# Copying transposed q and k out of PSUM in the order of the destination

## The chip, the cores and the metric

The kernel runs on one core of a Trainium2 chip. The metric is the device time of one execution in microseconds (us); several executions are timed and their median is compared.

## The reference

Two attentions over the same q, k and v (8 batches, 8 heads, 576 tokens, head size 64) are added, and the sum goes through a small network with a gated activation. One attention works on means of four neighbouring tokens (144 of them), the other only looks at keys fewer than 4 positions away.

```python
q_d = q.reshape(B, H, Sd, 4, D).mean(axis=3)          # k_d, v_d alike
out_d = sm_attn(q_d, k_d, v_d)
out_up = np.repeat(out_d, 4, axis=2)
mask = np.abs(pos[:, None] - pos[None, :]) < 4
scores = np.where(mask, scale * np.matmul(q, k.transpose(0, 1, 3, 2)), -1e9)
...
attn_out = out_up + out_local
x = attn_out.transpose(0, 2, 1, 3).reshape(B * S, H * D)   # 4608 x 512
h = x @ w_in                                               # 512 x 2048
return (h * (1 / (1 + np.exp(-h)))) @ w_out                # 2048 x 512
```

## The kernel before

**Work items.** The 64 heads are handled as 32 pairs (the two heads of a pair lie on partitions 0 to 63 and 64 to 127). For each pair p these tasks run:

- loads of q, k and v by SP's DMA queue; the tile `qs` holds six consecutive tokens per partition on 96 partitions;
- `cast`, to bf16 (`qb`, `kb`), on GpSimd (POOL), for the first four pairs on VectorE (DVE) and ScalarE (ACT);
- T (`ph_T`): TensorE (PE) transposes q in six pieces of 96 tokens into one PSUM bank and k into the neighbouring bank of a `duo` tile. Piece c holds the tokens 6g + c for g from 0 to 95, so the columns in PSUM stand in another order than the tokens. One VectorE instruction (L353) copies q to `qT`, one ScalarE instruction (L354) copies k to `kT`, both bf16 in SBUF, and both put the tokens in order on the way;
- `do_mean` (L362, L364), on VectorE: sums of two and then of four tokens of `qT` and `kT`, for the small attention;
- S1 and S2: scores by TensorE, and exponentials by ScalarE (L376, L391, L393);
- `do_mask` (L399), on VectorE;
- Z, once for two pairs: the sums of the exponentials on TensorE, copied to `zc` (ACT L423), sent by DMA into another shape (`zr`), inverted (`rr`, DVE L433), sent by DMA to DRAM (`scr`) and read back, broadcast over the partitions, as `Rb`. Pairs 2 and 3 take a direct way instead (L471);
- PV: the weighted values on TensorE, multiplied by `Rb` on VectorE (L488, L490) and added into `xT` (L507).

The network runs in 9 blocks of 512 tokens: g1 (TensorE into `hps`, then tanh on ScalarE at L530, then L532 on VectorE, which writes `gT`) and g2 (TensorE into `ops`, copied by ScalarE at L551, stored by SP). The two `duo` tiles are taken in turn by T, S1, S2, Z and PV; `hps` and `ops` have two buffers each.

**Order.** A planner in Python writes the order of each engine's instructions before the launch. It gives every operation a cost in nanoseconds, and always takes the next task that is ready by those costs; L353 and L354 are planned with 800 and 700. On the chip each engine then runs its list in that order, and waits on semaphores where an operand comes from another engine or a DMA.

Of the kernel before, what the change touches and what calls it, by code (L numbers as in the profile page):

```python
# [8 lines left out]
BF16 = mybir.dt.bfloat16  # L9
# [168 lines left out]
def bass_hourglass_attn__then__act_silu_kernel(  # L178
# [9 lines left out]
    with kctx:  # L188
# [4 lines left out]
        def R(name, psum=False):  # L193
            if name not in res:
                res[name] = Res(name, psum)
            return res[name]

        def sb(name, shape, dt, n=1):
            ts = [E(nc.sbuf_tensor(f"{name}{i}", shape, dt)) for i in range(n)]
            return ts if n > 1 else ts[0]  # L200
# [19 lines left out]
        qT = sb("qT", [128, S_], BF16, 2)  # L220
        kT = sb("kT", [128, S_], BF16, 2)
# [105 lines left out]
        def next_duo():  # L327
            d = nph[0] % 2
            nph[0] += 1
            return duo[d], [R(f"duo{d}a", True), R(f"duo{d}b", True)]  # L330
# [10 lines left out]
        def ph_T(p):  # L341
            D, bk = next_duo()
            j = p % 2
            for x, (nm, st) in enumerate((("q", qb), ("k", kb))):
                tps = D[:, x, 0:288].bitcast(BF16)
                for c in range(6):
                    w = st[j][:, c, :, :].rearrange("p h d -> p (h d)")
                    P.op("PE", lambda t, c=c, w=w, tps=tps: t.transpose(  # L348
                        tps[:, 96 * c:96 * c + 96], w, id_bf[:, :]),
                        r=[R("id"), R(f"{nm}b{j}")], w=[bk[x]], cost=42)  # L350
            src = [D[:, x, 0:288].bitcast(BF16).rearrange("p (r g) -> p r g", r=6) for x in range(2)]
            dst = [t[j][:, :].rearrange("p (g r) -> p r g", r=6) for t in (qT, kT)]
            P.op("DVE", lambda e: e.tensor_copy(dst[0], src[0]), r=[bk[0]], w=[R(f"qT{j}")], cost=800)  # L353
            P.op("ACT", lambda e: e.activation(dst[1], src[1], AF.Copy), r=[bk[1]], w=[R(f"kT{j}")], cost=700)  # L354

# [236 lines left out]
        for p in range(NPAIR):  # L592
            i, j, m, n, u = p % NST, p % 2, p % NP_, p % NVB, p % NR
# [22 lines left out]
            elif p % 2 == 1:  # L616
                task(side, f"r{z}", "DVE", [f"Z{z}"], [R(f"zr{z % 2}")], [], lambda z=z: do_recip(z))
                task(side, f"b{z}", chain(z), [f"r{z}", nm("PV", p - 1 - NR), nm("PV", p - NR)],
                     [R(f"scr{z % 2}")], [R(f"Rb{(p - 1) % NR}"), R(f"Rb{u}")], lambda z=z: do_bcast(z))
            task(attn, f"T{p}", "PE", [f"c{p}", nm("S2", p - 2)], [R(f"qb{j}"), R(f"kb{j}")], duo_w,  # L620
                 lambda p=p: ph_T(p))
            task(attn, f"S1{p}", "PE", [f"T{p}", nm("PV", p - NP_)], [R(f"qT{j}"), R(f"kT{j}")], duo_w,
                 lambda p=p: ph_S1(p), "row")
# [80 lines left out]
        while attn or side or g2n[0] < 16 * NSUP:  # L704
# [10 lines left out]
            if ready:  # L715
                ready.sort(key=lambda c: (c[2][6] != mode[0], c[1]))
                t = ready[0][2]
# [56 lines left out]
```

## Time and profile before

| | us |
|---|---|
| median of 3 runs (lowest to highest) | 443.34 (441.7 to 447.06) |
| the profiled execution | 443.05 |
| its span, first to last instruction | 441.0 |
| busy in the span: PE, DVE, ACT, POOL | 357.3, 329.6, 236.9, 157.7 |
| mean clock granted to TensorE, as a share of full speed | 0.965 |

Busy shares over the whole span mix three parts: a start of about 60 us without the network, a middle in which both attentions and the network run side by side, and an end from about 320 us on which holds little but the network. They are read apart, by windows.

### The profile page before, as it was taken

The page shows a single profiled execution, that of the slowest core. Times are in us where ns is not written, and L with a number is a line of the kernel's source. Part 1 is how long each engine was busy: PE and PEld are TensorE (multiplying, and loading weights), DVE is VectorE, ACT ScalarE, POOL GpSimd, SP SyncE. Part 2 cuts the span into 40 slices and gives each one's busy share as a digit, 9 for nine tenths or more (in the row PEclk, how much of TensorE's full clock was granted, in tenths as well). Part 3 has the DMA queues.
Part 4 walks back from the last instruction along what each step waited for, and adds up shares of the span by engine and source line. Part 5 has one row for each costly group of instructions (what it writes and reads, how often), then busy time and mean ns, then how long its engine had stood idle before and what let it go on. Part 6 is the DMA issues. An engine that isn't in the chain of part 4 may idle for free.

```text
span 441.0 us, 6955 instructions
## 1 busy us (share of the span) xinstructions
PE 357.3 (81%) x2688; PEld 211.4 (48%) x2688; DVE 329.6 (75%) x469; ACT 236.9 (54%) x328; POOL 157.7 (36%) x181
## 2 busy tenths in 40 slices
PE   3332278686859868889789989999999999999997
PEld 2211154352446544455445555555556555555553
DVE  5998399659789998999999999999966634333330
ACT  5830246623748638747468686767654243434331
POOL 4591637406354543262762746445110000000000
PEclk9999998978958999989999999999999999999999
DMA  6999999946756796484879887653205110010111
GB/s 182 229 304 298 205 210 230 220 120 167 197 133 149 210 216 161 143 210 124 205 164 230 207 209 175 194 175 87 92 27 159 51 48 25 24 49 24 48 49 71
DMA packets 81086, 66.38 MB, mean 151 GB/s; under 512 B 47006, under 2 KB 70558, under 8 KB 81054
## 3 DMA queue, kind: packets, MB, share of 16 engines
q1 hardware_dynamic: 75480, 57.38, 52.2%
q0 software_dynamic: 4224, 6.29, 5.9%
q10 hardware_dynamic: 1350, 2.28, 2.1%
q8 instruction: 21, 0.34, 0.4%
q14 instruction: 11, 0.09, 0.1%
HBM read 58.25 MB, written 9.61 MB: 154 GB/s over the span
## 4 chain that ended last, share of the span: by engine, by line
PE 46%; DVE 34%; ACT 10%; DMA 5%; issue 3%; ACTq 1%; POOL 1%; POOLq 0%
PE hps L338 21%; PE ops L338 19%; DVE qT L353 8%; DVE gT L532 6%; DVE hs L362 5%; ACT kT L354 5%; PE duo L338 4%; DVE Pt L399 3%; ACT th L530 3%; DVE xT L507 3%; DVE xo L488 3%; DVE qd L364 2%; DMA Rb<-scr 2%; PE duo L348 2%; DVE kd L364 1%
## 5 line engine op out<-in xcount | busy, mean ns | idle before, releaser
L338 PE MATMUL hps<-xT,w_in_sb 128*128 128x512 f32 x576 | 180.7, 441 | 10.9 <-DVE gT L532 10.5
L532 DVE SCALAR_TENSOR_TENSOR gT<-th,hps 128x512 bf16<-128x512 f32 x144 | 97.6, 687 | 73.1 <-ACT th L530 73.0
L338 PE MATMUL ops<-w_out_bf,gT 128*128 128x512 bf16 x576 | 149.3, 389 | 0.0
L530 ACT ACTIVATE th<-hps 128x512 f32<-128x512 f32 x144 | 88.9, 623 | 103.2 <-PE hps L338 96.8
L338 PEld LDWEIGHTS hps<-xT,w_in_sb 128*128 128x128 f32 x576 | 109.0, 196 | 46.2 <-DVE gT L532 12.2
L354 ACT ACTIVATE kT<-duo 128x576 bf16<-128x576 bf16 x32 | 67.8, 2120 | 23.8 <-DVE qT L353 12.4
L338 PEld LDWEIGHTS ops<-w_out_bf,gT 128*128 128x128 bf16 x576 | 47.3, 99 | 68.2 <-issue 26.3
L353 DVE COPY qT<-duo 128x576 bf16<-128x576 bf16 x32 | 66.6, 2082 | 2.9 <-PE duo L348 2.9
L317 POOL CAST vb<-vs 128x640 bf16<-128x640 f32 x32 | 27.0, 845 | 70.7 <-PE duo L338 46.5
L312 POOL CAST qb<-qs 96x768 bf16<-96x768 f32 x28 | 25.3, 903 | 74.7 <-PE duo L348 69.7
L319 POOL TENSOR_TENSOR vt<-vq 72x512 f32<-72x512 f32 x32 | 43.1, 1348 | 11.2 <-DMA vq<-in_v_dram 11.2
L338 PE MATMUL duo<-qT,kT 64*128 64x112 bf16 (+1 forms) x320 | 22.1, 233 | 21.9 <-ACT kT L354 9.5
L376 ACT ACTIVATE Pt<-duo 128x912 bf16<-128x912 f32 x32 | 30.9, 965 | 8.3 <-PE duo L338 7.6
L551 ACT ACTIVATE osb<-ops 128x512 f32<-128x512 f32 x36 | 21.7, 604 | 23.2 <-PE ops L338 19.6
L507 DVE TENSOR_TENSOR xT<-xo 128x576 fp32r<-128x576 f32 (+2 forms) x40 | 31.7, 808 | 1.1
L321 POOL TENSOR_TENSOR vd<-vt 72x256 bf16<-72x256 f32 x32 | 29.4, 918 | 4.1
L338 PEld LDWEIGHTS duo<-qT,kT 64*128 64x128 bf16 x320 | 11.7, 101 | 39.0 <-issue 13.2
L399 DVE TENSOR_TENSOR Pt<-Pt,mask_bf 128x1152 bf16<-128x1152 bf16 x32 | 28.9, 904 | 1.5 <-ACT Pt L391 1.5
L391 ACT ACTIVATE Pt<-duo 128x240 bf16<-128x240 f32 x32 | 12.4, 388 | 29.5 <-PE duo L338 23.8
L348 PE MATMUL duo<-id_bf,qb 96*128 96x96 bf16 x192 | 15.6, 225 | 14.4 <-POOL xo L273 4.8
L488 DVE TENSOR_TENSOR xo<-duo,Rb 128x456 f32<-128x456 f32 x32 | 19.9, 623 | 8.6 <-DMA Rb<-scr 7.6
L312 POOL CAST kb<-ks 96x768 bf16<-96x768 f32 x28 | 24.5, 877 | 1.7 <-DMA ks<-in_k_dram 1.7
(49 smaller groups left out, 273.5 us busy)
## 6 DMA issues: line engine op xcount, KB each, us to landing
vs<-in_v_dram SPq DMA_DIRECT2D x64, 160.0 KB, 4.2
qs<-in_q_dram SPq DMA_DIRECT2D x32, 288.0 KB, 4.9
ks<-in_k_dram SPq DMA_DIRECT2D x32, 288.0 KB, 5.6
vq<-in_v_dram SPq DMA_DIRECT2D x32, 288.0 KB
out_dram<-osb SPq DMA_DIRECT2D x36, 256.0 KB, 2.2
Rb<-scr SPq DMA_DIRECT2D x48, 180.0 KB, 3.6
w_in_sb<-in_moe_w_in_dram POOLq DMA_DIRECT2D x4, 1024.0 KB, 12.2
Rb<-scr ACTq DMA_DIRECT2D x12, 180.0 KB, 3.7
```

Of the source, the lines that this page charges most:

```text
L312: pool(lambda g, d=dst, s=src: g.tensor_copy(d, s), r=[R(f"{nm}s{i}")], w=[R(f"{nm}b{j}")], cost=830)
L319: pool(lambda g: g.tensor_tensor(vt[:, :, :], vq[i][:, :, 0:128], vq[i][:, :, 128:256], ALU.add), r=[R(f"vq{i}")], w=[R("vt")], cost=1290)
L321: pool(lambda g: g.tensor_tensor(vd[m][:, :, :], vt[:, :, 0:64], vt[:, :, 64:128], ALU.add), r=[R("vt")], w=[R(f"vd{m}")], cost=750)
L338: return P.op("PE", lambda t: t.matmul(out_, lhsT, rhs, start=start, stop=stop, skip_group_check=True), r, w, cost=cost)
L353: P.op("DVE", lambda e: e.tensor_copy(dst[0], src[0]), r=[bk[0]], w=[R(f"qT{j}")], cost=800)
L354: P.op("ACT", lambda e: e.activation(dst[1], src[1], AF.Copy), r=[bk[1]], w=[R(f"kT{j}")], cost=700)
L376: P.op("ACT", lambda e: e.activation(Pt[m][:, :, 0:456], D[:, :, 0:456], AF.Exp, scale=0.125), r=bk, w=[R(f"P{m}")], cost=930)
L399: P.op("DVE", lambda e: e.tensor_tensor(Pt[m][:, :, :], Pt[m][:, :, :], mask_bf[:, :].unsqueeze(1).to_broadcast([128, 2, S_]), ALU.mult), ...
L488: P.op("DVE", lambda e: e.tensor_tensor(xo[x][:, 0:456], D[:, 0, 0:456], Rb[u][:, 0:456], ALU.mult), r=[bk[0], R(f"Rb{u}")], w=[R(f"xo{x}" ...
L507: P.op("DVE", lambda e, dst=dst, in0=in0, in1=in1: e.tensor_tensor(dst, in0, in1, ALU.add), r=[R(f"xo{x}")], w=xblk(kc, t, e_), cost=180 + n)
L530: P.op("ACT", lambda e: e.activation(th[tb][:, :], hps[hb][:, :], AF.Tanh, scale=0.5), r=[R(f"h{hb}", True)], w=[R(f"th{tb}")], cost=600)
L532: P.op("DVE", lambda e: e.scalar_tensor_tensor(gT[j % 2][:, f, :], th[tb][:, :], 1.0, hps[hb][:, :], ALU.add, ALU.mult), r=[R(f"h{hb}", Tr ...
```

## The change

The two copies take the same elements to the same places; only the order in which an instruction walks through them differs. Before, the loop ran over the six pieces outside and the 96 tokens of a piece inside: consecutive elements are neighbours in PSUM (2 bytes apart), and land six elements (12 bytes) apart in SBUF. After, it runs over the 96 groups outside and the six pieces inside: consecutive elements are 96 elements (192 bytes) apart in PSUM and neighbours in SBUF. The planned costs are the same, and so each engine's list is the same, instruction for instruction; only the shapes of these two operands differ.

```diff
-            src = [D[:, x, 0:288].bitcast(BF16).rearrange("p (r g) -> p r g", r=6) for x in range(2)]
-            dst = [t[j][:, :].rearrange("p (g r) -> p r g", r=6) for t in (qT, kT)]
+            src = [D[:, x, 0:288].bitcast(BF16).rearrange("p (r g) -> p g r", r=6) for x in range(2)]
+            dst = [t[j][:, :].rearrange("p (g r) -> p g r", r=6) for t in (qT, kT)]
             P.op("DVE", lambda e: e.tensor_copy(dst[0], src[0]), r=[bk[0]], w=[R(f"qT{j}")], cost=800)
             P.op("ACT", lambda e: e.activation(dst[1], src[1], AF.Copy), r=[bk[1]], w=[R(f"kT{j}")], cost=700)
```

## Rows read from the trace of the kernel before

**Rows 1.** The page: busy times, then busy tenths in 40 slices of 11 us.

```profile
PE 357.3 (81%) x2688; PEld 211.4 (48%) x2688; DVE 329.6 (75%) x469; ACT 236.9 (54%) x328; POOL 157.7 (36%) x181
...
PE   3332278686859868889789989999999999999997
...
DVE  5998399659789998999999999999966634333330
...
DMA  6999999946756796484879887653205110010111
```

**Rows 2.** Windows of the span: busy us by engine, granted clock, DMA share, GB/s.

```profile
core 0: us, PE busy (x) PEld busy (x) DVE busy (x) ACT busy (x) POOL busy (x), PEclk, DMA share, GB/s
0.00:60.00 60.00, 17.81 (x219) 11.94 (x219) 44.00 (x55) 23.59 (x26) 32.40 (x51) 1.00 1.06 242
60.00:100.00 40.00, 32.61 (x209) 20.59 (x210) 30.43 (x41) 23.74 (x33) 18.00 (x21) 0.87 0.91 192
100.00:140.00 40.00, 28.91 (x273) 16.55 (x271) 34.62 (x44) 22.68 (x28) 20.30 (x21) 0.79 0.70 174
140.00:200.00 60.00, 49.79 (x425) 30.24 (x424) 55.73 (x82) 37.46 (x52) 26.84 (x30) 0.97 0.69 174
...
60.00:260.00 200.00, 164.26 (x1373) 98.46 (x1374) 178.06 (x247) 124.58 (x167) 96.14 (x102) 0.92 0.76 183
260.00:320.00 60.00, 57.92 (x503) 33.52 (x503) 56.91 (x91) 41.62 (x57) 27.44 (x28) 1.00 0.54 149
```

**Rows 3.** The page: the chain that ended last, shares of the span by line.

```profile
PE hps L338 21%; PE ops L338 19%; DVE qT L353 8%; DVE gT L532 6%; DVE hs L362 5%; ACT kT L354 5%; PE duo L338 4%; DVE Pt L399 3%; ACT th L530 3%; DVE xT L507 3%; DVE xo L488 3%; DVE qd L364 2%; DMA Rb<-scr 2%; PE duo L348 2%; DVE kd L364 1%
```

**Rows 4.** The two copies: durations in ns, min/median/max, first and last start.

```profile
L353 DVE COPY qT<-duo x32: 2016/2089/2122, 5.5 to 313.8; 128x576 bf16<-128x576 bf16 x32
...
L354 ACT ACTIVATE kT<-duo x32: 2082/2125/2154, 6.8 to 313.3; 128x576 bf16<-128x576 bf16 x32
```

**Rows 5.** Groups by shape: contiguous reads of PSUM on ACT and DVE (busy us, mean ns).

```profile
L376 ACT ACTIVATE Pt<-duo 128x912 bf16<-128x912 f32 x32 | 30.9, 965 | 8.3 <-PE duo L338 7.6 <-issue 0.3
...
L393 ACT ACTIVATE Pd<-duo 72x576 bf16<-72x576 f32 x32 | 20.5, 642 | 0.0
L488 DVE TENSOR_TENSOR xo<-duo,Rb 128x456 f32<-128x456 f32 x32 | 19.9, 623 | 8.6 <-DMA Rb<-scr 7.6 <-PE duo L338 1.0
...
L490 DVE TENSOR_TENSOR xo<-duo,Rb 128x264 f32<-128x264 f32 x32 | 13.4, 420 | 0.0
L391 ACT ACTIVATE Pt<-duo 128x240 bf16<-128x240 f32 x32 | 12.4, 388 | 29.5 <-PE duo L338 23.8 <-PE ops L338 3.7 <-PE duo L348 1.9
```

**Rows 6.** PE's waits from 60 to 260 us: total us, times, longest us.

```profile
PE hps L338 <- DVE gT L532: 9.7, 9, 3.3
PE duo L338 <- DVE xo L488: 7.5, 3, 3.1
PE duo L338 <- DVE qT L353: 6.5, 7, 3.1
PE duo L348 <- DVE qT L353: 3.9, 3, 1.7
...
PE duo L338 <- ACT kT L354: 1.5, 2, 0.9
```

**Rows 7.** Groups by shape on DVE from 60 to 260 us.

```profile
L353 DVE COPY qT<-duo 128x576 bf16<-128x576 bf16 x21 | 43.9, 2088 | 1.6 <-PE duo L348 1.6
```

**Rows 8.** Timeline of DVE in the start: start us, duration us, instruction, idle before.

```profile
5.51 2.08 DVE L353 COPY qT<-duo 128x576 bf16<-128x576 bf16 x1 [0.82 <-PE duo L348]
...
23.06 2.07 DVE L353 COPY qT<-duo 128x576 bf16<-128x576 bf16 x1
...
52.23 0.63 DVE L488 TENSOR_TENSOR xo<-duo,Rb 128x456 f32<-128x456 f32 x1 [7.59 <-DMA Rb<-scr]
```

**Rows 9.** Timeline of ACT and DVE: one round of denominators, from its copy to its use.

```profile
138.30 0.77 ACT L423 ACTIVATE zc<-duo 128x720 f32<-128x720 f32 x1
...
155.21 0.62 DVE L488 TENSOR_TENSOR xo<-duo,Rb 128x456 f32<-128x456 f32 x1
```

## Prediction

> **What bounds the kernel now.** I read the busy shares first, then windows, then the chain of waits, then PE's own waits. The slices [rows 1] show three parts. In the first five slices PE is busy a third of the time or less, DVE often 9 tenths, and the DMA engines 9 tenths nearly all the time. From there to about slice 28 DVE stands at 9 with few exceptions, and PE at 6 to 9. In the last eleven slices PE is at 9 and DVE at 3: that end is pure matrix work, holds no copy of q or k (the last starts at 313.8 us, [rows 4]), and the change can't touch it.
>
> The windows put numbers to this [rows 2]. From 60 to 260 us PE is busy 164.3 of 200 us (82%) and DVE 178.1 (89%); from 260 to 320 us PE is busy 57.9 of 60 (96.5%), so that this piece is already bound by TensorE although DVE has 56.9. What can be won lies mainly between 60 and 260 us, where PE idles 35.7 us. PE's waits there [rows 6] nearly all end on DVE: on `gT` 9.7 us, on the first product of PV 7.5, on the copy of q itself 6.5 + 3.9, and on ScalarE's copy of k only 1.5. DVE is in order and late, so whichever of its instructions PE needs is late; it is the bound of this stretch. The chain that ended last agrees [rows 3]: 8% of the span on L353 and 5% on L354, together 57 of 441 us.
>
> **The copies, one by one.** A copy of 576 elements takes 2089 ns on DVE and 2125 ns on ACT [rows 4]. What would it take at the full rate? From the contiguous reads of PSUM [rows 5]: on DVE 456 elements take 623 ns and 264 take 420, so (623 - 420) / 192 = 1.057 ns an element and 141 ns fixed, and 576 would take 750 ns. On ACT (965 - 388) / 672 = 0.859 ns an element and 182 ns fixed, so 677 ns. Turned round, the present copies cost (2089 - 141) / 576 = 3.38 ns an element on DVE and (2125 - 182) / 576 = 3.37 on ACT. Two engines with different rates of their own meet the same figure: the limit lies in how a memory is walked, not in the engine. The one odd thing about these instructions is the write of 2 bytes in every 12. That it is the write is my reading; no row shows a contiguous bf16 read of PSUM, so the read isn't cleared by itself.
>
> After the change the write is contiguous. The row for such a write is ACT's exponential into `Pd`: 576 bf16 elements a partition in 642 ns [rows 5], full rate. The read then steps 192 bytes, and no row shows a stepped read of PSUM. Its bounds: 750 and 677 ns if the step is free; as much as now, or more, if it costs what the stepped write costs. I take the lower end, since contiguous PSUM reads of several lengths all run at the engine's own rate, and both engines reach it. The saving is then 1.34 us of DVE and 1.45 us of ACT for each pair.
>
> [...]
>
> **The sum.** The profiled execution took 443.05 us, 2.05 outside its span, and the median of the runs is 443.34; I count from 443.05.
>
> *60 to 260 us.* 21 copies of q start here [rows 7], and as many of k. DVE's busy time falls by 21 x 1.339 = 28.1 to 149.9 us. If DVE kept its share of 89%, the stretch would last 168.4 us. But PE would then be busy 164.3 / 168.4 = 97.5%, more than the 96.5% of the densest stretch; at 96.5% it lasts 170.2 us. PE becomes the bound. I take 95.5%, 172 us, since the waits on `gT`, which come through ScalarE's tanh, won't all go. That is a gain of 28 us. ACT gives back 21 x 1.45 = 30 us of 124.6, but PE hardly waits on it, so I add nothing. The bounds of this term: at the least the waits that end on the copies themselves, 6.5 + 3.9 + 1.5 = 11.9 us; at the most all idle time and some clock. The granted clock was 0.87, 0.79 and 0.97 from 60 to 100, 100 to 140 and 140 to 200 us [rows 2]. [...]
>
> *260 to 320 us.* PE idles 2.1 us; I take nothing.
>
> *0 to 60 us.* Four copies of q, from 5.51 to 23.06 us, lie on DVE ahead of the first denominators [rows 8], 4 x 1.34 = 5.4 us. Behind them stand three transfers one after another, and the first product starts only at 52.23 us, after DVE idled 7.6 us for one of them, while the DMA engines are busy 9 tenths [rows 1]. An earlier start of a transfer into full engines comes back in part; between 0 and 5.4 I take 3.
>
> Sum: 28 + 3 = 31, so **412 us**. The chain gives a check from above: 35.3 us of L353 shrinks by 64%, 22.1 us of L354 by 68%, together 37.6 if nothing else came last; 31 is some four fifths of it. With the ends of each term (17 from 60 to 260 us if PE only gets to 90%, and 43 there) this case alone spans 396 to 425.
>
> **The rivals.** *A stepped read that costs part of it.* For it: consecutive elements are never neighbours in PSUM after the change. Against: nothing in the rows, they hold no such read. Halfway between the ends a copy takes 1420 ns and saves 0.67: DVE falls by 14.1 to 164.0 us, 184.3 us at its 89%, a gain of 15.7, and 1.5 in the start: 426 us, with 420 to 432 around it.
>
> *The denominators' round takes over.* From `zc` to the product that uses it 16.9 us go by in one round [rows 9], mostly transfers that a faster copy doesn't shorten. Some ten rounds lie between 60 and 260 us; 172 us give each 17.2. For it: that is close. Against: in 60 to 260 us PE's listed waits are on DVE's products late in DVE's list, and `Rb` held DVE back only in the start. If rounds come to 18 us, the stretch lasts 180: with 2 in the start, 421 us. It decides from rounds over 17.2 us on.
>
> *Nothing happens.* The 3.4 ns belong to 2-byte elements out of PSUM and not to the order of the write. For it: no row shows bf16 read out of PSUM in another way. 443 us.
>
> *Slower: the stepped read costs more than the stepped write.* A hop of 192 bytes at each element instead of 12. At 5 ns an element a copy takes 3.02 us, 0.93 more; 21 of them are 19.6 us on the engine that bounds the stretch, 22 us at its 89%, and 4 x 0.93 in the start: 469 us. It decides at 2.4 us a copy (0.32 more, some 9 us in all), 3.9 ns an element. Against: a walk through one bank of PSUM would have to be worse than one through SBUF.
>
> **How the numbers follow.** A measurement of this kernel tells about 2% from no change, so faster means below 434.5 us and slower above 452.2. Chances: forecast 0.60, partial price 0.17, denominators 0.07, nothing 0.09, slower 0.07. Faster is the first three but for a tail of 0.01: 0.83; the same 0.10; slower 0.07. The range takes the first three cases but for the thin end below 399 (much of the lower clock recovered) and leaves out the last two: 399 to 431.
>
> **What would show it.** L353 and L354 near 750 and 680 ns (right), near 1.4 us (the second case), unchanged or above 2.4 us (the last two). PE from 60 us to the last copy at 93% or more, with its waits on L353 gone and the rest short; a last copy of q near 283 us instead of 314; the pure end as long as before. If DVE idles on `Rb` or `zr` in many rounds, the third case holds. The forecast is wrong at its root if the copies fall to 750 ns and PE's share stays near 82%: then DVE was not the bound that I take it for.

## Result, and the profile after

The change makes the kernel faster: 421.82 us (421.47 to 422.9, 4 runs) against 443.94 us (441.7 to 447.06, 4 runs), a ratio of 0.950 with a 95% interval of 0.944 to 0.956. The forecast was 412 us, with 399 to 431 around it. The sign and the mechanism were right, the size was not: 21.2 us between the two profiled executions (443.05 and 421.84 us) where 31 were worked out.

The two copies first, in the kernel after (durations in ns, min/median/max, first and last start):

```profile
L353 DVE COPY qT<-duo x32: 683/750/758, 5.5 to 293.3; 128x576 bf16<-128x576 bf16 x32
...
L354 ACT ACTIVATE kT<-duo x32: 642/650/656, 6.7 to 292.8; 128x576 bf16<-128x576 bf16 x32
```

They answer to [rows 4]. The medians are 750 ns on DVE and 650 on ACT, where 750 and 677 were worked out from contiguous reads of f32: with a step of 192 bytes in PSUM the copies run at that rate.

The page of the kernel after, busy times, slices and chain:

```profile
PE 351.5 (84%) x2650; PEld 214.0 (51%) x2688; DVE 295.3 (70%) x469; ACT 195.6 (47%) x328; POOL 158.9 (38%) x181
...
PE   3503286868859969999799999999999999999996
...
DVE  5955799559788888998987989979948334333320
...
DMA  7999999967667795596979896733323100101011
...
PE 61%; DVE 15%; DMA 12%; ACT 4%; issue 3%; SPq 2%; ACTq 2%; POOL 1%; POOLq 0%
PE hps L338 27%; PE ops L338 25%; PE duo L338 6%; DMA Rb<-scr 5%; PE duo L348 4%; DMA scr<-rr 4%; DMA zr<-zc 3%; DVE hs L362 3%; DVE xT L507 2%; DVE xo L488 2%; DVE gT L532 2%; DVE qd L364 1%; ACT th L530 1%; ACTq L427 1%; DVE kd L364 1%
```

Against [rows 1] PE gets up to 9 from about slice 13 on, but the first twelve slices look much as before. L353 and L354 have gone from the chain of [rows 3]; in their place stand PE's own work and the three transfers of the denominators, 12% together.

To compare equal work, the span is cut where the network begins (60.92 us before, 54.53 after) and where the last copy of q begins (313.79 and 293.26). Windows before, then after; columns as in [rows 2]:

```profile
0.00:61.00 61.00, 18.81 (x231) 12.94 (x231) 44.97 (x57) 23.71 (x26) 32.40 (x51) 1.00 1.06 241
61.00:314.00 253.00, 215.78 (x1806) 128.27 (x1805) 228.07 (x328) 161.71 (x218) 122.14 (x127) 0.94 0.72 176
314.00:441.00 127.00, 122.72 (x655) 70.24 (x654) 56.52 (x87) 51.47 (x85) 3.19 (x3) 1.00 0.16 56
```

```profile
0.00:54.50 54.50, 18.56 (x230) 12.83 (x231) 37.87 (x56) 16.88 (x26) 31.72 (x49) 1.00 1.07 249
54.50:293.40 238.90, 211.03 (x1782) 130.91 (x1806) 201.69 (x328) 128.49 (x218) 124.08 (x130) 0.94 0.79 191
293.40:419.80 126.40, 121.89 (x644) 70.30 (x654) 55.75 (x87) 50.23 (x85) 3.10 (x3) 1.00 0.16 57
```

The start gave 6.5 us, the middle 14.1 and the end 0.6. In the middle PE idles 27.9 us of 238.9 where it idled 37.2 of 253; DVE is busy 84% of it, so it isn't the bound all along any more. The starts of the copies of q (numbered from 0) show where the middle's gain came. From copy 5 to copy 9 the stretch went from 39.2 us (61.65 to 100.89) to 40.2 (57.41 to 97.59): nothing gained. From copy 9 to copy 31 it went from 213.0 to 195.8 us: 17.2 gained over 22 copies, where 22 x 1.34 = 29.5 us were taken off DVE.

What DVE does in the stretch that gained nothing, on its timeline in the kernel after, with GpSimd's behind it (start us, duration us, instruction, idle before):

```profile
66.25 1.95 DVE L364 TENSOR_TENSOR qd<-hs 128x144 bf16<-128x144 f32 x1
68.12 2.21 DVE L362 TENSOR_TENSOR hs<-kT 128x288 f32<-128x288 bf16 x1
70.37 2.92 DVE L364 TENSOR_TENSOR kd<-hs 128x144 bf16<-128x144 f32 x1
...
90.18 0.59 DVE L433 RECIPROCAL rr<-zr 40x72 f32<-40x72 f32 x1 [1.62 <-DMA zr<-zc]
...
93.46 0.31 DVE L364 TENSOR_TENSOR qd<-hs 128x144 bf16<-128x144 f32 x1
```

```profile
68.75 1.27 POOL L319 TENSOR_TENSOR vt<-vq 72x512 f32<-72x512 f32 x1
70.10 0.83 POOL L321 TENSOR_TENSOR vd<-vt 72x256 bf16<-72x256 f32 x1
70.88 0.81 POOL L312 CAST qb<-qs 96x768 bf16<-96x768 f32 x1
71.64 0.82 POOL L312 CAST kb<-ks 96x768 bf16<-96x768 f32 x1
72.41 0.71 POOL L317 CAST vb<-vs 128x640 bf16<-128x640 f32 x1
```

An addition of 144 elements takes 0.31 us at 93 us, with GpSimd idle from 86.33 to 95.35 us, and 2.92 us at 70 us, while GpSimd runs one instruction after another; the one at 70.37 ends at 73.29, just behind the last of GpSimd's row at 73.12. And at 90 us DVE waits for the transfer into `zr`, which was issued from 80.27 to 83.31 us into full DMA engines (their share is 1.05 from 80 to 85 us).

### The profile page after: what moved, and what is told of

Same layout as the page of the kernel before. It is cut to its first block, busy times and chain, and to the rows that moved or that the text cites. A ratio compares the mean times of both kernels' runs of the same rounds, so it can differ in the third digit from the quotient of the medians.

```text
span 419.8 us, 6917 instructions
## 1 busy us (share of the span) xinstructions
PE 351.5 (84%) x2650; PEld 214.0 (51%) x2688; DVE 295.3 (70%) x469; ACT 195.6 (47%) x328; POOL 158.9 (38%) x181
## 4 chain that ended last, share of the span: by engine, by line
PE 61%; DVE 15%; DMA 12%; ACT 4%; issue 3%; SPq 2%; ACTq 2%; POOL 1%; POOLq 0%
PE hps L338 27%; PE ops L338 25%; PE duo L338 6%; DMA Rb<-scr 5%; PE duo L348 4%; DMA scr<-rr 4%; DMA zr<-zc 3%; DVE hs L362 3%; DVE xT L507 2%; DVE xo L488 2%; DVE gT L532 2%; DVE qd L364 1%; ACT th L530 1%; ACTq L427 1%; DVE kd L364 1%
## 5 line engine op out<-in xcount | busy, mean ns | idle before, releaser
L338 PE MATMUL hps<-xT,w_in_sb 128*128 128x512 f32 x576 | 184.2, 448 | 10.0 <-DVE gT L532 10.0
L530 ACT ACTIVATE th<-hps 128x512 f32<-128x512 f32 x144 | 85.9, 597 | 123.3 <-PE hps L338 119.9
L338 PE MATMUL ops<-w_out_bf,gT 128*128 128x512 bf16 x538 | 139.3, 384 | 3.9 <-issue 2.5
L338 PEld LDWEIGHTS hps<-xT,w_in_sb 128*128 128x128 f32 x576 | 112.0, 200 | 43.8 <-DVE gT L532 9.8
L507 DVE TENSOR_TENSOR xT<-xo 128x576 fp32r<-128x576 f32 (+2 forms) x40 | 33.6, 856 | 1.1
L376 ACT ACTIVATE Pt<-duo 128x912 bf16<-128x912 f32 x32 | 29.7, 927 | 7.9 <-PE duo L338 7.9
L321 POOL TENSOR_TENSOR vd<-vt 72x256 bf16<-72x256 f32 x32 | 31.7, 991 | 4.1
L354 ACT ACTIVATE kT<-duo 128x576 bf16<-128x576 bf16 x32 | 20.8, 649 | 26.7 <-DVE qT L353 13.5
L399 DVE TENSOR_TENSOR Pt<-Pt,mask_bf 128x1152 bf16<-128x1152 bf16 x32 | 30.7, 959 | 0.8 <-ACT Pt L391 0.8
L353 DVE COPY qT<-duo 128x576 bf16<-128x576 bf16 x32 | 23.7, 740 | 2.4 <-PE duo L348 2.3
```

What stands on the lines that cost most here:

```text
L321: pool(lambda g: g.tensor_tensor(vd[m][:, :, :], vt[:, :, 0:64], vt[:, :, 64:128], ALU.add), r=[R("vt")], w=[R(f"vd{m}")], cost=750)
L338: return P.op("PE", lambda t: t.matmul(out_, lhsT, rhs, start=start, stop=stop, skip_group_check=True), r, w, cost=cost)
L376: P.op("ACT", lambda e: e.activation(Pt[m][:, :, 0:456], D[:, :, 0:456], AF.Exp, scale=0.125), r=bk, w=[R(f"P{m}")], cost=930)
L399: P.op("DVE", lambda e: e.tensor_tensor(Pt[m][:, :, :], Pt[m][:, :, :], mask_bf[:, :].unsqueeze(1).to_broadcast([128, 2, S_]), ALU.mult), ...
L507: P.op("DVE", lambda e, dst=dst, in0=in0, in1=in1: e.tensor_tensor(dst, in0, in1, ALU.add), r=[R(f"xo{x}")], w=xblk(kc, t, e_), cost=180 + n)
L530: P.op("ACT", lambda e: e.activation(th[tb][:, :], hps[hb][:, :], AF.Tanh, scale=0.5), r=[R(f"h{hb}", True)], w=[R(f"th{tb}")], cost=600)
```

## Experiments

The ratio given with each is to the kernel before, on the same chip in the same runs; the change alone has 0.950 (0.944 to 0.956).

### One copy at a time

```diff
# q_only: L353 as after, L354 as before.  k_only: the reverse.
-            src = [....rearrange("p (r g) -> p g r", r=6) for x in range(2)]
+            src = [....rearrange(f"p (r g) -> p {o}", r=6) for x, o in enumerate(("g r", "r g"))]
```

> Only the copy of q (DVE, L353) walks in the order of the destination; the copy of k stays as before. Theory A, DVE was the bound of the middle and PE waited 10.4 us on the copy of q but 1.5 us on that of k: L353 750 ns, L354 2.1 us, 425 to 429 us, three quarters of the gain or more. Rival, the chain's shares decide (35 us of q, 22 of k): 60% of the gain, about 431 us.

> Only the copy of k (ACT, L354) walks in the order of the destination. Theory A: the middle stays bound by DVE, L354 650 ns, 438 to 441 us, a gain of 3 to 6 us mostly in the start. Rival, the chain's shares decide: about 435 us.

q alone: 432.57 us, ratio 0.975 (0.969 to 0.982). k alone: 440.82 us, ratio 0.993 (0.988 to 0.997). Neither theory got both: q gave half of the gain, not three quarters, and so came near the 431 us of the rival; k gave the little that theory A said. The two are worth 2.5% and 0.7% apart and 5.0% together. The start shows one reason. There the two copies of a pair run side by side on two engines, and the scores need both. The second, third and fourth copy of q start at 10.10, 14.90 and 23.06 us before; at 10.13, 14.94 and 20.48 with q alone; at 9.68, 14.35 and 23.07 with k alone; at 8.79, 12.26 and 16.14 with both. In the middle DVE no longer is the only late one with q alone: ACT's copies still take a median of 2121 ns, and from 60 to 300 us DVE sits idle for ACT's tanh (L530) for 36.6 us, where with both copies changed it is 26.1. That ACT's longer list is the whole of the missing gain is argued, not shown.

### What the step of the write and of the read cost

```diff
# steps_write (o = "r g") and steps_read (o = "g r"): step by pair
+            n = (1, 2, 3, 4, 6, 8, 16, 32)[p % 8]      # steps_read: (1, 2, 6, 18, 36, 72, 144, 288)
+            src = [....rearrange(f"p (r g) -> p {o}", r=n) for x in range(2)]
+            dst = [t[j][:, :].rearrange(f"p (g r) -> p {o}", r=n) for t in (qT, kT)]
```

> The copies of q and k read PSUM in order and write SBUF in steps of 2, 4, 6, 8, 12, 16, 32 and 64 bytes, in turn by pair, so tokens lie in a wrong order. Theory A, the write's step made the old copies slow: full rate at 2 bytes (about 0.65 us on ACT, less than 0.75 on DVE), 2.1 us at 12 bytes; where in between the cost sets in is not known. Rival, 2-byte elements out of PSUM are slow by themselves unless hopped: 2.1 us at every step.

> The copies of q and k write SBUF in order and read PSUM in steps of 2, 576, 192, 64, 32, 16, 8 and 4 bytes, in turn by pair, so tokens lie in a wrong order. Theory A, a stepped read of PSUM costs nothing at any step: 0.75 us on DVE and 0.65 on ACT throughout, with DVE less at 2 bytes if it then takes two elements at a time. [...]

The copies of q in steps_write, from its timeline on DVE; the steps of these eight are 2, 4, 6, 8, 12, 16, 32 and 64 bytes:

```profile
238.72 0.45 DVE L353 COPY qT<-duo 128x576 bf16<-128x576 bf16 x1
251.22 0.79 DVE L353 COPY qT<-duo 128x576 bf16<-128x576 bf16 x1
253.09 1.13 DVE L353 COPY qT<-duo 128x576 bf16<-128x576 bf16 x1
267.40 1.38 DVE L353 COPY qT<-duo 128x576 bf16<-128x576 bf16 x1
272.60 2.11 DVE L353 COPY qT<-duo 128x576 bf16<-128x576 bf16 x1
283.63 2.68 DVE L353 COPY qT<-duo 128x576 bf16<-128x576 bf16 x1
292.20 2.64 DVE L353 COPY qT<-duo 128x576 bf16<-128x576 bf16 x1
306.54 2.73 DVE L353 COPY qT<-duo 128x576 bf16<-128x576 bf16 x1
```

Less the 141 ns taken as fixed, these are an estimated 0.54 ns an element at 2 bytes, 1.13 at 4, 2.15 at 8, 3.42 at 12 and 4.41 at 16, about in proportion to the step, and no more than that at 32 and 64 (4.34 and 4.49). ACT's copies agree: 0.65, 0.82, 1.15, 1.47, 2.13, 2.77, 2.69 and 2.78 us. The four copies of each step agree within 0.11 us on either engine. In steps_read the copies of DVE took 0.45 us at 2 bytes and 0.68 to 0.76 us at every step from 4 to 576 bytes; those of ACT took 0.64 to 0.66 us at all of them, 2 bytes too. Four of DVE's, at steps of 2, 576, 8 and 4 bytes:

```profile
223.14 0.45 DVE L353 COPY qT<-duo 128x576 bf16<-128x576 bf16 x1
...
236.79 0.75 DVE L353 COPY qT<-duo 128x576 bf16<-128x576 bf16 x1
...
275.86 0.75 DVE L353 COPY qT<-duo 128x576 bf16<-128x576 bf16 x1
...
289.08 0.75 DVE L353 COPY qT<-duo 128x576 bf16<-128x576 bf16 x1
```

So the write made the old copies slow, both engines alike: at its 12 bytes steps_write has 2.00 to 2.11 us on DVE and 2.08 to 2.13 on ACT. A stepped read of PSUM cost ACT nothing (0.64 to 0.66 us); it cost DVE about the 0.30 us by which the read in order is faster (0.45 us against 0.68 to 0.76), about the same at every step: at 4 bytes and at 8 the median is 0.75 us. Each of the two kernels ran once; of their times only the copies are used.

### Plain order on both sides

```diff
-            src = [D[:, x, 0:288].bitcast(BF16).rearrange("p (r g) -> p g r", r=6) for x in range(2)]
-            dst = [t[j][:, :].rearrange("p (g r) -> p g r", r=6) for t in (qT, kT)]
+            src = [D[:, x, 0:288].bitcast(BF16) for x in range(2)]
+            dst = [t[j][:, :] for t in (qT, kT)]
```

> Both copies read and write in plain order (tokens stay in the order of the pieces, which is wrong). Theory A, the step of the read costs nothing on ACT (0.65 us, as with the step) and DVE has little left to give: L353 0.45 us or 0.75, and 418 to 422 us. Rival, the stepped read still costs something that the kernel pays: below 416 us.

419.89 us, ratio 0.943 (0.935 to 0.950), L353 at a median of 448 ns and L354 at 650. DVE's copy is 0.30 us shorter again, 9.7 us over 32 of them, and little of it arrives: the intervals of the two ratios overlap. PE itself had little left to wait for there: its matmuls waited on L353 for 2.2 us in all in the kernel after, and for 13.1 us before.

### Where the rest of the gain went

Three kernels take one hindrance each from the changed kernel, and a fourth takes two.

```diff
# no_round: VectorE waits for no transfer of the denominators, and reads a constant tile
+        if eng == "DVE": drop waits on the transfers into Rb and zr
-                rr[i] = 1 / zr[i];  xo = D * Rb[u]
+                rr[i] = 1 / Rbc[0:40, 0:72];  xo = D * (Rb[u] if p in direct else Rbc)
# small_pool: from the sixth pair on
-            vt[:, :, :] = vq[i][:, :, 0:128] + vq[i][:, :, 128:256];  vd[m] = vt[:, :, 0:64] + vt[:, :, 64:128]
+            the same on 8 columns
# pool_memset: from the sixth pair on
+            memset(vt) in place of each of the two
# both: no_round and small_pool
```

> The changed kernel, in which VectorE waits neither for the denominators' transfer into zr nor for the broadcast Rb: it reads a constant tile in their place, so the denominators are left out except for pairs 2 and 3; all transfers still run, and the order is the same. Theory A, the round of transfers holds VectorE in the start (9.6 us idle), at about 90 us and at about 146 us: 410 to 416 us. Rival, these waits are covered by PE's other work: within 3 us of 421.8.

> The changed kernel, in which GpSimd's two additions for the means of v (L319, L321) work on 8 columns instead of 128 and 64 from the sixth pair on, so the means of v of later pairs are stale; order and waits are the same. Theory A, VectorE's instructions with two SBUF inputs (L362, L364, L399, L507) are held up while GpSimd's run, and this took back part of the gain: their means fall towards their shortest ones (0.45, 0.31, 0.75, 0.76 us) and the time to 408 to 415 us. Rival, VectorE has slack after the change and PE is held by other things: within 3 us of 421.8.

> The changed kernel, in which from the sixth pair on GpSimd's two additions for the means of v become two fills of a tile of about the same total length (2.1 us against 2.3), which read nothing; the means of v of later pairs are stale. Theory A, VectorE's instructions with two SBUF inputs are held up by GpSimd's reading: their means fall as in small_pool and the time to 413 to 417 us. Rival, small_pool gained because GpSimd's own list got shorter and its casts came earlier: 419 to 423 us, VectorE's means as with the change alone.

> small_pool and no_round together (denominators and later means of v left out). If the two hold up different stretches, their gains add: 404 to 408 us. Rival, both gained before the tenth pair, on the same stretch of 60 to 100 us, and the second finds little left: 409 to 413 us.

| | us | ratio to before |
|---|---|---|
| no_round | 413.66 | 0.928 (0.917 to 0.938) |
| small_pool | 414.29 | 0.935 (0.929 to 0.940) |
| pool_memset | 416.38 | 0.938 (0.932 to 0.944) |
| both | 405.64 | 0.913 (0.907 to 0.920) |

*GpSimd holds up DVE.* In pool_memset GpSimd is about as busy with its two instructions (0.95 us each in place of 1.35 and 0.99), but reads nothing in them. DVE's groups by shape from 60 to 300 us, in the kernel after and then in pool_memset:

```profile
L399 DVE TENSOR_TENSOR Pt<-Pt,mask_bf 128x1152 bf16<-128x1152 bf16 x26 | 23.8, 914 | 0.8 <-ACT Pt L391 0.8
...
L507 DVE TENSOR_TENSOR xT<-xo 128x576 fp32r<-128x576 f32 x15 | 17.0, 1132 | 0.5
...
L364 DVE TENSOR_TENSOR qd<-hs 128x144 bf16<-128x144 f32 x27 | 15.1, 558 | 0.9
L364 DVE TENSOR_TENSOR kd<-hs 128x144 bf16<-128x144 f32 x27 | 14.9, 551 | 0.9
```

```profile
L399 DVE TENSOR_TENSOR Pt<-Pt,mask_bf 128x1152 bf16<-128x1152 bf16 x27 | 22.5, 833 | 1.6 <-ACT Pt L391 1.6
...
L364 DVE TENSOR_TENSOR qd<-hs 128x144 bf16<-128x144 f32 x27 | 12.4, 461 | 0.9
...
L364 DVE TENSOR_TENSOR kd<-hs 128x144 bf16<-128x144 f32 x27 | 12.2, 451 | 0.9
L507 DVE TENSOR_TENSOR xT<-xo 128x576 fp32r<-128x576 f32 x16 | 12.1, 758 | 0.5
```

All groups with two inputs in SBUF fell but one (the sums from `kT`, 602 to 647 ns), together from 110.3 to 96.8 us, and the time with them, to 416.4 us (its interval and that of the change alone meet at 0.944). So what these two instructions read held DVE up, and the rival of pool_memset (419 to 423 us) falls. But it isn't small_pool's gain over again: the starts below show small_pool 8.0 us ahead of the change at copy 9 and pool_memset 1.3. Up to there most of small_pool's gain is something else; what is left for it is GpSimd's shorter list, between whose casts DVE gets free, and that is argued, not shown.

*The round.* no_round gained 8.2 us, all of it by copy 9 of q: that starts 8.3 us earlier than in the kernel after, and copy 30 the same 8.3 us. The starts of copies of q, in us:

| copy | before | after | no_round | small_pool | pool_memset | both |
|---|---|---|---|---|---|---|
| 5 | 61.65 | 57.41 | 50.73 | 56.46 | 56.95 | 50.39 |
| 9 | 100.89 | 97.59 | 89.25 | 89.64 | 96.25 | 89.41 |
| 10 | 115.20 | 109.79 | 104.95 | 104.20 | 107.13 | 101.95 |
| 30 | 299.44 | 280.04 | 271.72 | 273.90 | 274.70 | 263.91 |

Up to copy 9 no_round and small_pool each gain 8 us over the change, and both together no more: three kernels arrive at 89.2 to 89.6 us. For two of them, no_round and both, the chain of waits shows where this floor begins, at a load of v. In no_round (start us, us, what):

```profile
48.34 11.80 DMA vq<-in_v_dram
...
63.85 0.83 POOL qb L312
...
66.23 3.30 PE hps L338 x8
...
73.34 0.78 ACT zc L423
...
74.14 0.77 ACTq L427
```

GpSimd waits for that load until 60.1 us, and so its cast for copy 7 comes at 63.85 us (64.04 in both, where GpSimd waits for a load of v until 61.6); the DMA engines are busy 0.99 of the time from 60 to 100 us. Then the chain runs through ScalarE, which issues the four transfers into `zr` with the next tanh behind them: no_round frees VectorE from the round, not ScalarE. In small_pool the chain of this stretch runs over PE and DVE, so that it arrives at the same time can be chance. No run takes the loads away, so the floor is read from these chains and not tested.

From copy 9 to 30 the stretch is 182.5 us with the change, 182.5 in no_round, 184.3 in small_pool and 174.5 with both; neither gains alone there, together they gain 8. This hangs on the cut: counted from copy 10, they gain 3.5 and 0.6 us apart and 8.3 together, and pool_memset gains 2.7 alone. So the expectation that the two lie in different stretches, though its 404 to 408 us came true and the medians add up (8.2 and 7.5 us, 16.2 together), was wrong in its reason: up to copy 9 the two gain the same 8 us, and behind it they gain more together than apart. These are single executions, and those of no_round differ by up to 7.7 us.

### Three attempts at a faster kernel

```diff
# direct4
-        direct = (2, 3)
+        direct = (0, 1, 2, 3)
# costs: planned costs of L362, L364, L399, L507 540, 480, 900, 340 + n; of the copies 720, 650; a transfer's end 3600
# hs_psum: behind the two copies
+            for x in range(2): hs[x] = PSUM tokens 0, 2, 4 of each six + qT or kT tokens 1, 3, 5
```

> The changed kernel with pairs 0 and 1 on the direct way to their denominators too (as pairs 2 and 3 have it), so that no round of transfers is left in the start; the planner sets a new order. Theory A, the first round (26 us from its copy to its use) sets when the network starts: 412 to 418 us. Rival, the two more direct ways cost VectorE 9.7 us in the start, as much as the round's waits: 420 to 424 us.

> The changed kernel with planned costs nearer to the measured times of VectorE's instructions and of the transfers; the planner sets a new order. Theory A, part of the remaining waits of PE comes from an order planned with too short times: 412 to 419 us. Rival, the waits are VectorE's and the transfers' own, whatever the order: 419 to 425 us.

> The changed kernel with the first additions of the means (L362) right behind the copies, reading one token of each two from PSUM in steps and the other from qT or kT, so that only one input lies in SBUF. Theory A, they then no longer wait for GpSimd: 0.45 us each, and 414 to 419 us. Rival, the PSUM tile is held longer and TensorE waits for it: 421 to 427 us.

direct4: 422.12 us, ratio 0.950 (0.944 to 0.957), no gain; the figure is the rival's, but the waits name another reason. Its first round is gone, but PE and DVE then wait in the start for work that needs a load; waits of PE, in us, times, longest:

```profile
PE duo L348 <- POOL qb L312: 22.0, 3, 10.7
```

These casts stand in GpSimd's list behind the casts of v, and those waited 6.83 us for a load at 38.73 us and 4.39 at 57.12. It fits a floor that the loads set. costs: 425.29 us, ratio 0.957 (0.950 to 0.964); truer costs didn't make a better order. hs_psum: 417.76 us, ratio 0.940 (0.932 to 0.948). The additions behave as meant (durations in ns, min/median/max):

```profile
L354 DVE TENSOR_TENSOR hs<-duo,qT x32: 457/457/459, 6.4 to 299.6; 128x288 f32<-128x288 bf16 x32
...
L354 DVE TENSOR_TENSOR hs<-duo,kT x32: 447/448/458, 7.5 to 300.0; 128x288 f32<-128x288 bf16 x32
```

With the change alone they took 534 and 610 ns on average and up to 1630 and 2214; with one input in PSUM not one of the 64 took longer than 459. The planner made a new order here too, so the time isn't due to the additions alone. It has the lowest median of the kernels that compute all of the reference, but its interval overlaps that of the change: a gain of 1% is likely, not settled.

## Why the prediction was right in sign and too large

*The copies.* Right in what the sum needs: the write's step was the cost, and 750 ns were forecast and measured on DVE, 677 and 650 on ACT. But 750 ns are not DVE's full rate for bf16: in order on both sides it takes 448 ns (flat), and the rows of f32 behind my 750 could not show that. The second case, 1.4 us a copy, is out, as are the two cases with unchanged or longer copies.

The runs tell the step of the write from that of the read. A write on DVE took 0.45 us at 2 bytes, 2.68 at 16, and 2.64 and 2.73 at 32 and 64: its cost grew up to 16 bytes and not at 32 and 64. Reads of PSUM behaved otherwise: ACT took 0.64 to 0.66 us at every step, and DVE, which is at 0.45 us in order, 0.68 to 0.76 at every step from 4 to 576 bytes.

*The term of 60 to 260 us.* This is the step that failed in size: 28 us, where the middle from copy 5 to the last gave 16.3 (4.2 us earlier at copy 5, 20.5 at copy 31). I took the whole 200 us as bound by DVE, at one share of 89%. But [rows 2] show a first part, 60 to 100 us, with DVE busy only 30.4 of 40 us and the DMA engines 91%. There nothing was gained from shorter copies, while no_round and small_pool both pass it 8 us sooner. The step that followed, PE becomes the bound, didn't come true either: I had named 93% or more as its sign, and PE is busy 88% from the network's begin to the last copy (211.03 of 238.9 us; 85% before), DVE 84%, and the last copy of q starts at 293 us instead of 283. Neither engine bounds that stretch by itself.

*What DVE gave back.* I took DVE's other instructions at their old durations. Those with two inputs in SBUF (L362, L364, L399, L507) came to 133.0 us before and 137.8 after, summed over their groups by shape. At their medians in the kernel after, 0.45 us for L362, 0.31 for L364 and 0.75 for L399, and at the 0.76 us that L507 took on average in pool_memset, L362 to L507 for whole blocks would take 36.6 us less: 64 x 0.45, 64 x 0.31, 32 x 0.75 and 24 x 0.76 us against 127.5. That GpSimd's reading causes part of it pool_memset shows, where from 60 to 300 us they fell from 110.3 to 96.8 us. That it grew by 4.8 us is not explained by a run of its own. The old copies, with their one input in PSUM, may have been time in which GpSimd could read without holding DVE up; that is argued, not shown.

*The third case, the denominators' round,* came true in part, and I had given it 0.07. DVE waited for `Rb` from 145.0 to 146.1 and again for 0.33 us before 148.29, and PE was busy 2.39 of the 5 us from 145 to 150. The next window had a granted clock of 0.50, as the windows of the kernel after show:

```profile
145.00:150.00 5.00, 2.39 (x10) 1.25 (x10) 3.49 (x9) 1.19 (x2) 0.14 (x1) 0.97 0.98 217
150.00:155.00 5.00, 4.22 (x15) 2.80 (x16) 4.65 (x8) 1.00 (x2) 3.90 (x4) 0.50 1.05 205
```

But the round's main cost lay in the start and at 90 us, not in many rounds of the middle, as the case had it: no_round was 8.3 us ahead of the change at copy 9 and still 8.3 at copy 30. So that the 421 us of this case lie beside the measured 421.82 is no proof of it. The case itself was built on a weak row: the round that I read, 16.9 us, is the shortest of the nine that start between 60 and 260 us in the kernel before (the others take 17.8 to 25.0), and rounds overlap (one `zc` is written at 138.30 us, before the use of the one before it at 147.93). A length of 17.2 us was therefore not the limit that I made of it.

*The clock* gave nothing, as counted: 0.94 in the middle before and after. So no run shows the 43 us that the term of 60 to 260 us was given at its low end; the middle from copy 5 on gave 16.3.

*The start* gave 6.5 us to the network's begin where I took 3 out of 0 to 5.4. I had counted the copies of q alone. With both, the fourth copy starts 6.9 us earlier, and the first product with `Rb` at 44.00 us against 52.23 in [rows 8].

*The sums.* With the ends of both terms the forecast's own case spans 395 to 426 us, not 396 to 425; nothing hangs on it. *The check by the chain* was too kind: 37.6 us as a bound from above and four fifths of it as the answer. What came next on the chain, transfers and PE's own list, stood closely behind.

With both hindrances left out the kernel takes 405.6 us, below the forecast. That doesn't show that all of the 31 us would come through without them: no run leaves them out of the kernel before, where they may cost as much.

## What to carry to other kernels

When an engine reorders elements on their way from PSUM to SBUF, let the read do the stepping and write in order: here DVE took 2.09 us for 576 elements written 12 bytes apart, and 0.75 for the same read 192 bytes apart and written in order. A write cost more the farther apart its elements lay, up to 16 bytes (2.7 us), and no more at 32 and 64. Before a saving on a busy engine is turned into time, split its stretch where another resource is full (here the DMA engines, 0.91 busy from 60 to 100 us), and give each piece its own next bound. When one engine's list gets shorter, look at what its instructions run beside: here a copy that reads PSUM kept its time beside GpSimd (683 to 758 ns in all 32), an addition with two inputs in SBUF did not (0.31 to 2.92 us).

## What the runs showed of the hardware

- A bf16 write of 576 elements a partition into SBUF took 0.8, 1.1 to 1.2, 1.4 to 1.5, 2.0 to 2.1 and 2.7 to 2.8 us at steps of 4, 6, 8, 12 and 16 bytes, and 2.6 to 2.85 us at 32 and 64, on DVE and ACT alike. Less the fixed times of the prediction, 141 and 182 ns, that is an estimated 1.1 ns an element at 4 bytes and 4.3 to 4.6 at 16, 32 and 64, on both engines.
- Reads of 576 bf16 elements of PSUM in steps of 4 to 576 bytes, written in order, took 0.68 to 0.76 us on DVE, an estimated 0.94 to 1.07 ns an element without the fixed 141 ns; with 2-byte neighbours on both sides DVE took 0.45 us, an estimated 0.54 ns an element, and ACT 0.64 to 0.66 us in any case.
- An addition of 144 elements on DVE with two inputs in SBUF, 0.31 us when GpSimd was idle, took up to 2.92 us while GpSimd read without a pause. In pool_memset, where two of GpSimd's instructions only write from the sixth pair on, L364 on `kd` fell from 551 to 451 ns on average; in hs_psum, with one of the two inputs in PSUM, the sums of `kT` fell from 610 to 450 ns. In pool_memset GpSimd's casts still read, and the sums from `kT` did not get faster (602 to 647 ns).
- Two changes on parallel branches were worth more together than apart (2.5% and 0.7% against 5.0%), and so was leaving out two hindrances (3.5 and 0.6 us apart, 8.3 together, from copy 10 to 30 in one execution each).
